# Four moves in the two-tile phase of a tiled Fourier convolution: weight group, first tile's transform, third plane operation, third tile's planes

## The chip, the cores and the metric

The kernel runs on one core of a Trainium2 chip. The metric is the device time of one execution in microseconds, as the median over several runs. The core has five engines that matter here: TensorE (PE, with PEld for its weight loads), VectorE (DVE), ScalarE (ACT), GpSimd (POOL) and SyncE (SP, which here only issues DMAs).

## The reference

An image of 224x224 pixels with 96 channels is convolved, circularly, with 7x7 taps from 96 to 96 channels. The reference does it by Fourier transforms:

```python
wp = jnp.pad(w, ((0, H - K), (0, W - K), (0, 0), (0, 0)))
Xf = rfft2(x, axes=(1, 2)); Wf = rfft2(wp, axes=(0, 1))
Yf = jnp.einsum('bhwi,hwio->bhwo', Xf, Wf)
y = irfft2(Yf, s=(H, W), axes=(1, 2)).astype(bfloat16)
```

## The kernel before, in words

**Tiling.** The kernel does not form the two-dimensional transform. Down the height it cuts the image into 8 blocks of 28 rows (two halves, `jg`, of four blocks) and transforms each block with its halo by matmuls with a matrix that it builds itself (`Fm`); that gives 17 frequencies, `s` = 0 to 16. Across the width it convolves directly, with a saving: pixels are taken in pairs, and the sums and differences of neighbouring pixels (and of real and imaginary parts) need fewer multiplications. The width is cut into 7 tiles of 32 pixels (`t` = 0 to 6).

**Stages.** For a tile: (1) the transform of its pixels to `xf`, in PSUM banks that VectorE or ScalarE evicts; (2) the planes `J`, sums and differences of `xf` on VectorE; (3) a round for each frequency s, in which TensorE multiplies planes with the transformed weights `WF`; (4) the way back, matmuls with `Gm` on data that went through a scratch in DRAM (`scr`), and the stores to the output.

**Weights.** `WF` is made from the raw weights (`wq`) in six groups of frequencies, `PGRP` = (0,2), (2,5), (5,8), and so on. `prep_jobs(gi)` (line 337) gives the jobs of a group: twelve banks of four matmuls with an eviction each, and for each inner frequency one difference on VectorE (`diff`, WF<-WF). Group 0 is made ahead of the rounds.

**A round** is `b_round(t, s, mid, end, ydve, planes)` (line 493). It takes two PSUM banks. In the first TensorE does 4, 4 and 4 matmuls (on a J plane, then on `xf` twice) and then 7 on two more J planes; those 7 read what the third plane operation wrote. ScalarE copies a part of this bank out (tt), VectorE makes `u` from the rest. Then come the `mid` jobs, 14 matmuls into the second bank, VectorE's `v` from it, the plane operations that the round was given, the sum of u and v on GpSimd (`ysum`, yf<-v,u), and the `end` jobs. For s = 0 and 16 the round is shorter (8 and 14 matmuls, no GpSimd). Where a round was given plane operations, the sum on GpSimd is made to wait for the last of them (lines 571 to 577).

**Planes.** `jit(t, g)` (line 463) gives the three VectorE operations that make the planes of the frequency group `JGB[g]` of tile t: a wide subtraction, a small addition, and an addition that reads the result of the first. They go into one of three buffers J, in turn.

**Order.** Each engine runs its instructions in the order of the program (`_Ordered`). In the two-tile phase (lines 741 to 793) round r does frequency r of tile 0 and, from r = `LAG` = 4 on, frequency r-4 of tile 1 after it; so there are 21 rounds, of up to two half rounds. Which half round gets which planes stands in `bursts`, keyed by (r, t). Other work comes in through paced queues: `add(a, b, jobs)` spreads jobs evenly over the steps a to b-1, and `pace` (line 722) pops what is due at a step. The steps are 2r for the middle and 2r+1 for the end of a round while there is one tile, and 2r and 2r+1 for tile 0's and tile 1's half rounds where there are two. Queues are served in the order in which they were added, so weight groups come first. `f_jobs(t, part)` (line 441) gives a tile's transform in three parts by frequency, s 0 to 7, 8 to 12 and 13 to 16; `fj[1][1]` and `fj[2][1]` are the upper two parts of tile 0 for the second half of its rows, 4 banks of 8 matmuls and 2 banks of 16. The engine of an eviction is chosen as the program is built, by running sums of estimated costs (`evac`, line 119).

After the two-tile phase, tiles 2 to 6 go one at a time, with the next tile's transform and the way back of earlier tiles in between.

Of the kernel before, what the change touches and what calls it, by code (L numbers as in the profile page):

```python
# [17 lines left out]
NS = L // 2  # L18
# [14 lines left out]
PGRP = ((0, 2), (2, 5), (5, 8), (8, 11), (11, 14), (14, 17))  # L33
# [6 lines left out]
JGB = ((0, 3), (3, 6), (6, 9), (9, 12), (12, 15), (15, 17))  # L40
LAG = 4
# [14 lines left out]
def kernel(  # L56
# [406 lines left out]
    def jit(t, g):  # L463
        s0, s1 = JGB[g]
        n = s1 - s0
        xf = xf_tiles[t][0:C]
        xv = xf.rearrange("c p r s w j -> c p r s (w j)")
        b = jcount[0] % 3 if t < 2 else (jcount[0] - 2 * len(JGB)) % 2
        jcount[0] += 1
        Jb = J_bufs[b][0:C].rearrange("c (k s q) -> c k s q", k=7, s=3)  # L470
        for s in range(s0, s1):
            jbuf[(t, s)] = Jb[:, :, s - s0]

        def sub(o, a, b, op, cost):
            def f():
                load["v"] += 170 + cost / 1.92
                return VE.tensor_tensor(out=o, in0=a, in1=b, op=op)
            return f
        x0, x1 = xv[:, 0, :, s0:s1], xv[:, 1, :, s0:s1]
        c0, c1 = max(s0, REAL[0] + 1), min(s1, REAL[1])  # L480
        i0, i1 = c0 - s0, c1 - s0
        pd, rd, sd, qd = x1.ap
        dpl = bass.AP(x1.tensor, x1.offset - NJ, [pd, [NJ, 2], rd, sd, qd])
        return [
            sub(Jb[:, 0:4, 0:n].rearrange("c (k r) s q -> c k r s q", r=2), dpl,
                x0.unsqueeze(1).to_broadcast([C, 2, 2, n, PP]), ALU.subtract, 4 * PP * n),
            sub(Jb[:, 4, i0:i1], xv[:, 0, 0, c0:c1], xv[:, 0, 1, c0:c1], ALU.add, PP * (c1 - c0)),
            sub(Jb[:, 5:7, i0:i1], Jb[:, 0:4:2, i0:i1], Jb[:, 1:4:2, i0:i1], ALU.add, 2 * PP * (c1 - c0)),
        ]
# [3 lines left out]
    def b_round(t, s, mid, end, ydve=False, planes=()):  # L493
# [26 lines left out]
        if s in REAL:  # L520
            for part in range(2):
                conv(b0, part * C, 0, part)
            SE.copy(out=tt_[:, 0:2 * C], in_=b0[:, 0:2 * C])
            mid()
            for mi, m in enumerate((2, 1)):
                for part in range(2):
                    conv(b1, (mi * 2 + part) * C, m, part)
            VE.tensor_tensor(out=yv.rearrange("p r m o -> p m r o"),
                             in0=tt_[:, 0:2 * C].rearrange("p (r o) -> p r o", o=C).unsqueeze(1).to_broadcast([128, 2, 2, C]),
                             in1=b1[:, 0:4 * C].rearrange("p (m r o) -> p m r o", m=2, r=2), op=ALU.add)  # L530
            load["a"] += 110 + 0.9 * 192
            load["v"] += 540
            for f in planes:
                f()
            end()
        else:
            v = tv_pool.tile([128, 2, 2, C], F32, name="v")
            if merge:
                conv(b0, 2 * C, 0, 0, both=True)
                conv(b0, 2 * C, 2, 0, add=True)  # L540
                conv(b0, 3 * C, 1, 0, add=True)
                conv(b0, 0, 0, 1)
                conv(b0, C, 0, 2)
                SE.mul(out=tt_[:], in_=b0[:, 0:4 * C], mul=-0.5)
                u, pr = tt_[:, 2 * C:4 * C].rearrange("p (m o) -> p m o", m=2), tt_[:, 0:2 * C]
            else:
                for part in range(3):
                    conv(b0, part * C, 0, part)
                conv(b0, 3 * C, 2, 0)
                conv(b0, 4 * C, 1, 0)  # L550
                u = tv_pool.tile([128, 2, C], F32, name="u")
                SE.mul(out=tt_[:, 0:3 * C], in_=b0[:, 0:3 * C], mul=-0.5)
                pr = tt_[:, C:3 * C]
            if puts:
                puts.pop(0)()
            if not merge:
                VE.scalar_tensor_tensor(out=u[:], in0=b0[:, 3 * C:5 * C].rearrange("p (m o) -> p m o", m=2), scalar=-0.5,
                                        in1=tt_[:, 0:C].unsqueeze(1).to_broadcast([128, 2, C]), op0=ALU.mult, op1=ALU.add)
            mid()
            for mi, m in enumerate((2, 1)):  # L560
                for pi, part in enumerate((1, 2)):
                    conv(b1, (mi * 2 + pi) * C, m, part)
            VE.scalar_tensor_tensor(out=v.rearrange("p m r o -> p m (r o)"),
                                    in0=pr.unsqueeze(1).to_broadcast([128, 2, 2 * C]), scalar=-2.0,
                                    in1=b1[:, 0:4 * C].rearrange("p (m q) -> p m q", m=2), op0=ALU.mult, op1=ALU.add)
            def ysum(eng):
                return eng.tensor_tensor(out=yv.rearrange("p r m o -> p m r o"), in0=v[:],
                                         in1=u.unsqueeze(2).to_broadcast([128, 2, 2, C]), op=ALU.add)
            if ydve:
                ysum(VE)  # L570
            last = None
            for f in planes:
                last = f()
            if not ydve:
                y = ysum(GE)
                if last is not None:
                    tc.add_manual_dep(y.ins, last.ins.name, SYNC, reason="sum after planes")
            load["a"] += 490 if merge else 410
            load["v"] += (560 if ydve else 250 if t < 2 else 0) + (560 if merge else 900)
            end()  # L580
# [119 lines left out]
    fj = [f_jobs(0, p) for p in range(3)]  # L700
# [37 lines left out]
    def add(a, b, jobs):  # L738
        qs.append([a, b, jobs, len(jobs)])

    for gi in range(1, len(PGRP)):
        add(2 * PGRP[gi - 1][0], 2 * PGRP[gi - 1][1] - 1, prep_jobs(gi))
    for t in range(2):
        scr_tiles[t] = dr_pool.tile([TW, NJ, NS, 4 * C], BF16, name="scr")
    bursts = {}
    for g in range(len(JGB)):
        g0 = JGB[g][0]
        if g:
            bursts[(g0 - 2, 1 if g0 - 2 >= LAG else 0)] = (0, g)
        r1 = LAG + g0 - (3 if g == len(JGB) - 1 else 1)  # L750
        bursts[(r1, 0 if r1 < NS else 1)] = (1, g)
    bursts[(NS + LAG - 2, 1)] = (2, 0)
    nburst = len(bursts)
    for r in range(NS + LAG):
        if r == 0:
            add(0, 4, fj[1][1] + fj[2][1])
        for p in range(3):
            if r == (1, 3, 5)[p]:
                new_xf(1, SH2[p], SH2[p + 1])
                fj = f_jobs(1, p)  # L760
                if p == 2:
                    for jg in range(2):
                        fj[jg][-1] = then_load(fj[jg][-1], 2, jg)
                add(2 * r + 1, 2 * r + (5, 5, 4)[p], fj[0] + fj[1])
        for p in range(3):
            if r == SH2[p + 1] + 1 - (p == 2):
                new_xf(2, SH2[p], SH2[p + 1])
                fj = f_jobs(2, p)
                if p == 2:
                    for jg in range(2):  # L770
                        fj[jg][-1] = then_load(fj[jg][-1], 3, jg)
                add(2 * r, 2 * r + (8, 7, 5)[p], fj[0] + fj[1])
        if r == PGRP[-2][1] + 1:
            assert not any(q[2] for q in qs[:len(PGRP) - 1])
            wtmp_cm.__exit__(None, None, None)
            t_pool = ctx.enter_context(tc.tile_pool(name="tt", bufs=NTT, side="right"))
            t2_pool = ctx.enter_context(tc.tile_pool(name="tt2", bufs=1, side="right"))
            yo_pool = ctx.enter_context(tc.tile_pool(name="yo", bufs=2, side="right"))
            g_pool = ctx.enter_context(tc.tile_pool(name="gp", bufs=1, side="right"))
            GA = g_pool.tile([KA, 4 * B], BF16, name="GA")  # L780
            GB = g_pool.tile([128, 2, 4 * B], BF16, name="GB")
            GE.memset(GA[:], 0.0)
            GE.memset(GB[:], 0.0)
        if r == NS + 3:
            queue_c(0)
        for t in range(2):
            s = r - LAG * t
            if not 0 <= s < NS:
                continue
            now = bursts.pop((r, t), ())  # L790
            now = jit(*now) if now else ()
            both = LAG <= r < NS
            b_round(t, s, fills(qs, 2 * r + (t if both else 0)), fills(qs, 2 * r + (t if both else 1)), False, now)
    assert not bursts and nburst == 2 * len(JGB)
    if NP2:
        ps0_cm.__exit__(None, None, None)
        ps_cms = [tc.tile_pool(name="ps", bufs=NP2, space=bass.MemoryType.PSUM),
# [108 lines left out]
```

## Time and profile before

| | us |
|---|---|
| median of 3 runs | 271.96 (271.89 to 272.75) |
| the profiled execution's own time | 272.2 |
| its span, first to last instruction | 270.5 |
| TensorE busy | 258.7 (96%) |
| VectorE busy | 213.9 (79%) |
| ScalarE busy | 195.6 (72%) |
| GpSimd busy | 95.6 (35%) |

A row of a timeline gives the start in us, the length, the engine, a line of the kernel, the operation, what it writes and reads with shapes, the number of instructions merged into the row, and in brackets the idle time of the engine before it and what ended that. All instructions carry line 88, the helper that keeps the order, so they are told apart by the names of their tiles: `pb` is a PSUM bank, `WF<-pb` a weight eviction, `WF<-WF` a difference, `J<-xf` the first two plane operations, `J<-J` the third, `u`, `v`, `yf` as above. Rows of TensorE overlap, since matmuls are pipelined.

### The profile page before, as it was taken

The page shows a single profiled execution, that of the slowest core. Times are in us where ns is not written, and L with a number is a line of the kernel's source. Part 1 is how long each engine was busy: PE and PEld are TensorE (multiplying, and loading weights), DVE is VectorE, ACT ScalarE, POOL GpSimd, SP SyncE. Part 2 cuts the span into 40 slices and gives each one's busy share as a digit, 9 for nine tenths or more (in the row PEclk, how much of TensorE's full clock was granted, in tenths as well). Part 3 has the DMA queues.
Part 4 walks back from the last instruction along what each step waited for, and adds up shares of the span by engine and source line. Part 5 has one row for each costly group of instructions (what it writes and reads, how often), then busy time and mean ns, then how long its engine had stood idle before and what let it go on. Part 6 is the DMA issues. An engine that isn't in the chain of part 4 may idle for free.

```text
span 270.5 us, 12170 instructions
## 1 busy us (share of the span) xinstructions
PE 258.7 (96%) x5149; PEld 237.8 (88%) x5149; DVE 213.9 (79%) x457; ACT 195.6 (72%) x483; POOL 95.6 (35%) x156
## 2 busy tenths in 40 slices
PE   8899998999999999999999999999999999899983
PEld 3679898999999989999999999998998989789862
DVE  5647999898889888779787888787898889778623
ACT  5549997568875657988988889887887865477113
POOL 7781032435536624431422222223222242422100
PEclk9999999999999999999999999999999999999999
DMA  6947010731121498986977477989649834887766
GB/s 168 232 124 200 23 47 2 204 105 49 43 77 63 126 276 157 292 247 177 298 206 217 116 205 244 251 210 349 222 125 163 269 103 147 200 235 203 221 118 202
DMA packets 47014, 46.78 MB, mean 173 GB/s; under 512 B 35286, under 2 KB 37986, under 8 KB 46960
## 3 DMA queue, kind: packets, MB, share of 16 engines
q1 hardware_dynamic: 44672, 43.94, 58.7%
q10 hardware_dynamic: 2288, 2.06, 2.7%
q8 instruction: 40, 0.66, 1.1%
q14 instruction: 14, 0.11, 0.2%
HBM read 24.65 MB, written 21.33 MB: 170 GB/s over the span
## 4 chain that ended last, share of the span: by engine, by line
PE 74%; DVE 7%; DMA 7%; ACT 5%; issue 3%; POOL 2%; SPq 1%; DVEq 0%; POOLq 0%; ACTq 0%
PE pb L88 74%; DMA tt<-scr 4%; ACT WF L88 3%; POOL ct L88 2%; DMA xf<-scrb 2%; DVE J L88 2%; DVE v L88 1%; DVE WF L88 1%; DVE u L88 1%; ACT xf L88 1%; DMA scrb<-yf 1%; SPq L88 1%; DVE yf L88 1%; DVE xf L88 1%; DVE wq L88 1%
## 5 line engine op out<-in xcount | busy, mean ns | idle before, releaser
L88 PE MATMUL pb<-WF,J 96*128 96x96 bf16 x2821 | 162.5, 206 | 1.1 <-DVE J L88 0.6
L88 PEld LDWEIGHTS <-J 96*128 96x128 bf16 x2821 | 138.1, 98 | 10.4 <-issue 2.6
L88 POOL TENSOR_TENSOR yf<-v,u 128x384 bf16<-128x384 f32 x79 | 78.6, 1008 | 151.7 <-issue 88.6
L88 ACT CAST xf<-pb 96x408 bf16<-96x408 f32 (+3 forms) x144 | 67.3, 486 | 8.1 <-PE pb L88 6.2
L88 PE MATMUL pb<-WF,xf 96*128 96x96 bf16 x952 | 60.2, 206 | 0.8 <-ACT xf L88 0.5
L88 DVE TENSOR_TENSOR J<-xf 96x1824 bf16<-96x1824 bf16 (+1 forms) x84 | 57.6, 724 | 0.1
L88 PEld LDWEIGHTS <-xf 96*128 96x128 bf16 x952 | 47.1, 98 | 1.2 <-ACT xf L88 0.6
L88 PE MATMUL pb<-Fm,xn 118*128 118x136 bf16 (+3 forms) x640 | 45.5, 199 | 0.9 <-DVE u L88 0.8
L88 PE MATMUL pb<-tt,Gm 102*84 102x384 bf16 (+1 forms) x132 | 32.7, 327 | 1.7 <-DMA tt<-scr 1.7
L88 ACT CAST WF<-pb 96x480 bf16<-96x480 f32 (+1 forms) x59 | 29.0, 570 | 5.7 <-PE pb L88 5.7
L88 PEld LDWEIGHTS <-xn 118*128 118x128 bf16 x640 | 30.4, 97 | 1.1 <-issue 1.1
L88 ACT CAST J<-pb 84x384 bf16<-84x384 f32 (+1 forms) x64 | 27.6, 488 | 2.4 <-PE pb L88 2.3
L88 ACT CAST yo<-pb 84x384 bf16<-84x384 f32 (+1 forms) x64 | 27.2, 482 | 1.9 <-PE pb L88 1.1
L88 DVE TENSOR_TENSOR J<-J 96x912 bf16<-96x912 bf16 (+2 forms) x42 | 22.8, 542 | 0.0
L88 PE MATMUL pb<-wq 98*128 98x120 bf16 (+1 forms) x288 | 21.3, 225 | 0.0
L88 PEld LDWEIGHTS <-wq 98*128 98x128 bf16 x288 | 19.5, 149 | 0.2
L88 PE MATMUL pb<-wu 128*128 128x512 bf16 (+1 forms) x80 | 17.6, 381 | 1.0 <-DVE ct L88 1.0
L88 PEld LDWEIGHTS <-wu 128*128 128x128 bf16 (+1 forms) x80 | 9.3, 118 | 8.2 <-issue 2.4
L88 DVE TENSOR_TENSOR yf<-v,u 128x384 bf16<-128x384 f32 x26 | 14.7, 566 | 0.9
L88 PEld LDWEIGHTS <-Gm 102*84 102x84 bf16 (+1 forms) x132 | 11.0, 117 | 2.7 <-DMA tt<-scr 2.1
L88 DVE CAST WF<-pb 96x480 bf16<-96x480 f32 (+1 forms) x13 | 7.5, 610 | 5.4 <-PE pb L88 5.3
L88 ACT COPY xf<-xf 96x816 bf16<-96x816 bf16 (+3 forms) x20 | 11.2, 618 | 0.0
(386 smaller groups left out, 233.4 us busy)
## 6 DMA issues: line engine op xcount, KB each, us to landing
scr<-yf SPq DMA_DIRECT2D x30, 288.0 KB
xn<-in_x_dram SPq DMA_DIRECT2D x12, 672.0 KB
tt<-scr SPq DMA_DIRECT2D x24, 336.0 KB
out_dram<-yo SPq DMA_DIRECT2D x12, 252.0 KB
out_dram<-J SPq DMA_DIRECT2D x12, 252.0 KB
tt<-scr SPq DMA_DIRECT2D x6, 288.0 KB
WF<-in_x_dram SPq DMA_DIRECT2D x2, 672.0 KB
out_dram<-tt SPq DMA_DIRECT2D x8, 168.0 KB
```

Source lines behind the costliest of these rows:

```text
L88: r = fn(*a, **k)
```

## The change

Four places of the two-tile phase are edited.

1. The second weight group (gi = 1, frequencies 2 to 4) is spread over two steps, 0 and 1, instead of three; the other groups keep theirs.
2. Tile 0's upper transform for the second half of the rows: the 4 banks of the middle part are spread over steps 1 to 4 and the 2 banks of the top part over steps 5 to 8, instead of all 6 over steps 0 to 3.
3. Of the three plane operations of a group, the half round that starts the group does two; the third is kept in `rest` and done at the same place of the next half round. The sum on GpSimd waits for planes only where more than one was done in its half round.
4. The planes of tile 2's first group start one round sooner: two operations in round 18 and the third in round 19, instead of all three in round 19.

```diff
             if not ydve:
                 y = ysum(GE)
-                if last is not None:
+                if len(planes) > 1:
                     tc.add_manual_dep(y.ins, last.ins.name, SYNC, reason="sum after planes")
...
     for gi in range(1, len(PGRP)):
-        add(2 * PGRP[gi - 1][0], 2 * PGRP[gi - 1][1] - 1, prep_jobs(gi))
+        add(2 * PGRP[gi - 1][0], 2 * PGRP[gi - 1][1] - (2 if gi == 1 else 1), prep_jobs(gi))
...
     bursts = {}
+    rest = []
...
-    bursts[(NS + LAG - 2, 1)] = (2, 0)
+    bursts[(NS + LAG - 3, 1)] = (2, 0)
...
         if r == 0:
-            add(0, 4, fj[1][1] + fj[2][1])
+            add(1, 5, fj[1][1])
+            add(5, 9, fj[2][1])
...
             now = bursts.pop((r, t), ())
-            now = jit(*now) if now else ()
+            now = jit(*now) if now else []
+            now, rest = rest + now[:2], now[2:]
             both = LAG <= r < NS
             b_round(t, s, fills(qs, 2 * r + (t if both else 0)), fills(qs, 2 * r + (t if both else 1)), False, now)
-    assert not bursts and nburst == 2 * len(JGB)
+    assert not rest and not bursts and nburst == 2 * len(JGB)
```

## Prediction

> **What bounds the kernel now.** I read the chain of waits, busy time by stage, then TensorE's timeline in the stretch where two tiles run together (21 to 98 us).
>
> ```profile
> PE 74%; DVE 7%; DMA 7%; ACT 5%; issue 3%; POOL 2%; SPq 1%; DVEq 0%; POOLq 0%; ACTq 0%
> ```
> ```profile
> 61.20:97.70 36.50, 35.86 (x879) 35.62 (x879) 30.71 (x63) 26.56 (x64) 19.23 (x21) 1.00 0.28 89
> 97.70:270.50 172.80, 165.43 (x3143) 152.17 (x3143) 135.03 (x289) 125.96 (x323) 49.27 (x50) 1.00 0.76 209
> ```
> TensorE makes up 74% of the chain that ends last, and its clock is 1.00. In both stretches it is busy nearly throughout (columns: length; PE, PEld, DVE, ACT, POOL; clock). The change leaves TensorE's work alone; it can only remove or add standstills. What comes after 97.7 us has the same work and order, so I carry a standstill saved before it to the end whole. The standstills (start, length, group, idle time before it and its releaser):
>
> ```profile
> 29.20 0.33 PE L88 MATMUL pb<-WF,J 96*128 96x96 bf16 x4 [0.36 <-DVE WF L88]
> 29.37 0.33 PE L88 MATMUL pb<-WF,xf 96*128 96x96 bf16 x4
> 29.89 0.33 PE L88 MATMUL pb<-WF,xf 96*128 96x96 bf16 x4 [0.19 <-DVE WF L88]
> ...
> 45.71 0.95 PE L88 MATMUL pb<-Fm,xn 118*128 118x32 bf16 x32 [0.80 <-DVE u L88]
> ...
> 57.97 0.94 PE L88 MATMUL pb<-wq 98*128 98x120 bf16 x12
> 58.75 0.93 PE L88 MATMUL pb<-WF,J 96*128 96x96 bf16 x18
> 59.52 0.50 PE L88 MATMUL pb<-WF,xf 96*128 96x96 bf16 x8
> 59.85 0.46 PE L88 MATMUL pb<-WF,J 96*128 96x96 bf16 x7
> 60.15 0.92 PE L88 MATMUL pb<-wq 98*128 98x120 bf16 x12
> 61.17 0.39 PE L88 MATMUL pb<-Fm,xn 118*128 118x64 bf16 x8
> ```
> ```profile
> 88.53 0.46 PE L88 MATMUL pb<-WF,J 96*128 96x96 bf16 x7
> ...
> 96.58 0.50 PE L88 MATMUL pb<-WF,xf 96*128 96x96 bf16 x8
> 97.70 0.94 PE L88 MATMUL pb<-WF,J 96*128 96x96 bf16 x18 [0.62 <-DVE J L88]
> ```
> Matmuls overlap: eight last 0.50, but the next group starts after 0.33 (59.52 to 59.85). So a standstill is the bracketed idle time plus about 0.16. Round 2 of tile 0 waits for its weights: 0.36+0.16 = 0.52 and 0.19+0.16 = 0.35. At 45.71 TensorE waits 0.80+0.16 = 0.96 for a PSUM bank that u frees. From 60.15 to 61.17 are 1.02 where twelve such matmuls took 0.78 before: 0.24. Tile 2's first round waits 1.12-0.33 = 0.79 for its planes. Together 2.86; smaller ones I leave out.
>
> **The change part by part.** VectorE's rows for all parts, and one of GpSimd's:
>
> ```profile
> 27.67 0.36 DVE L88 SCALAR_TENSOR_TENSOR u<-pb,tt__681 128x192 f32<-128x192 f32 x1 [1.61 <-ACT tt__681 L88]
> ...
> 29.19 1.80 DVE L88 TENSOR_TENSOR WF<-WF 96x960 bf16<-96x960 bf16 x3
> 30.90 0.55 DVE L88 SCALAR_TENSOR_TENSOR v<-tt__681,pb 128x384 f32<-128x384 f32 x1
> ...
> 39.51 2.54 DVE L88 TENSOR_TENSOR WF<-WF 96x960 bf16<-96x960 bf16 x3
> ...
> 45.32 0.34 DVE L88 SCALAR_TENSOR_TENSOR u<-pb,tt__1168 128x192 f32<-128x192 f32 x1
> ...
> 58.95 0.62 DVE L88 TENSOR_TENSOR J<-J 96x912 bf16<-96x912 bf16 x1
> 59.49 0.34 DVE L88 SCALAR_TENSOR_TENSOR u<-pb,tt__1601 128x192 f32<-128x192 f32 x1
> 59.76 0.54 DVE L88 SCALAR_TENSOR_TENSOR v<-tt__1601,pb 128x384 f32<-128x384 f32 x1
> 60.76 0.36 DVE L88 SCALAR_TENSOR_TENSOR u<-pb,tt__1662 128x192 f32<-128x192 f32 x1 [0.46 <-POOL yf L88]
> ```
> ```profile
> 39.40 1.00 POOL L88 TENSOR_TENSOR yf<-v,u 128x384 bf16<-128x384 f32 x1 [3.67 <-DVE J L88]
> ```
> ```profile
> 87.67 0.62 DVE L88 TENSOR_TENSOR J<-J 96x912 bf16<-96x912 bf16 x1
> 88.22 0.34 DVE L88 SCALAR_TENSOR_TENSOR u<-pb,tt__2546 128x192 f32<-128x192 f32 x1
> 88.48 0.53 DVE L88 SCALAR_TENSOR_TENSOR v<-tt__2546,pb 128x384 f32<-128x384 f32 x1
> ...
> 95.81 0.36 DVE L88 SCALAR_TENSOR_TENSOR u<-pb,tt__2867 128x192 f32<-128x192 f32 x1 [1.22 <-ACT tt__2867 L88]
> 96.09 0.55 DVE L88 SCALAR_TENSOR_TENSOR v<-tt__2867,pb 128x384 f32<-128x384 f32 x1
> 96.55 1.32 DVE L88 TENSOR_TENSOR J<-xf 96x1824 bf16<-96x1824 bf16 x2
> ```
> Second weight group: its fifteen jobs (twelve banks, three differences) go out 8 and 7 in two steps instead of 5, 5, 5 in three. The differences (29.19 to 30.90, 1.71 in the queue) now stand ahead of round 1's u at 27.67, before which VectorE idled 1.61. I expect them to fill that hole: u perhaps 0.3 later, everything behind them 1.71-0.3, about 1.4, earlier. Round 2 then finds its weights: 0.52+0.35 = 0.87 saved; nothing if the casts run late on ScalarE, which released that u.
>
> First tile's upper transform: the same six banks and matmuls, but one at a time from the end of round 0 to round 3 instead of all in rounds 0 and 1. TensorE does them without loss whenever they come. What is late next is their eviction, into stretches where VectorE has work without a gap. For two late banks that is 0 to 1.1 of VectorE's time (an estimate: 0.54, like v, for each). I take 0, since the lead worked out next just covers the bank wait at 45.71; at 1.1 about that wait, 0.96, would stay. No DMA hangs on these jobs; SyncE's and GpSimd's queues keep their order.
>
> Third operation, gain: on VectorE it took from 58.95 to 59.49, 0.54 of the queue, ahead of the u that frees a bank. Behind that round's v instead, it lets u go 0.54 sooner. At 45.32, u comes 1.4+0.54 = 1.94 sooner while TensorE asks 0.87 sooner, so 1.07 is there to cover 0.96: all saved (nothing, if the hole stays). The sum on GpSimd, which waits for the planes where there are two or more, also starts 0.54 sooner; that covers the 0.46 of the u at 60.76: 0.24 saved.
>
> Third operation, cost: one half round later it stands close to its reader, the seven matmuls on J. In tile 0's fourth group, v would run from 59.22, leave the queue at 59.68, and the operation end at 59.68+0.62 = 60.30; its reader stands at 59.85: 0.45 late. GpSimd also gets in the way. Three differences took 2.54 at 39.51 with a sum on GpSimd from 39.40 to 40.40, and 1.80 alone: 0.74 lost of 0.89 shared. Here tile 1's sum would run from about 59.1 to 60.1, so the operation ends near 60.65: **0.8 late**; with tile 0's sum ahead of it too, 1.75; bounds 0.45 and 1.75. Tile 1's fifth group: u from 87.68, v from 87.94, the operation from 88.40 to 89.02 against a reader at 88.53: 0.5 late, 0.7 with the rest of a sum in front, at most 1.75. I take **0.7**. The other groups have no row for the new place; each lies between 0 and the operation's own 0.62. I take 0.3 for all of them, near the low end, because the other tile's half round lies between the operation and its reader. Cost 1.8; bounds 0.95 (0.45+0.5) and 4.1 (1.75+1.75+0.62).
>
> The Trainium skill, "SBUF — State Buffer", section "Who interferes with whom", says a vector operation with two SBUF inputs and a GpSimd operation that reads SBUF exclude each other, whichever issued first holding on to its end. The row at 39.51 agrees (0.74 of 0.89). By that rule a third operation right behind v would go ahead of the sum and pay nothing itself, which no run here shows; the fourth group would then stay at 0.8, since there a sum is already running.
>
> Third tile's planes: the first two operations of tile 2, 1.32 at 96.55, move one round forward, ahead of the u at 95.81. There VectorE idles 1.22, waiting for ScalarE. So they are hidden but for 0.1, and 0.79 is saved; should the hole vanish, u and its bank slip by up to 1.32. The sum of that round then waits for them, but nothing queues behind it that tile 2's first round reads.
>
> Sum: 0.87+0.96+0.24+0.79-1.8 = 1.06 saved. The profiled execution took 272.2 (span 270.5, 1.7 around it), so 271.1; the runs' median, 271.96, is 0.24 lower, so **270.9**.
>
> **The rivals.**
> - The planes are always in time: the hand sums above put the third operation too late, because VectorE, relieved of its backlog, is ahead everywhere. For it: 1.4 saved early. Against: u at 60.76 shows VectorE waiting again later, so the lead does not last. All 2.86: 269.1.
> - The saving is handed to the next wait. For it: from 29.19 to 45.32 VectorE's rows have no gap, so TensorE, sooner at one wait, may stand longer at the next; then 0.96 and 0.24 stay and, of the other 1.66, the third operations take 1.2 to 1.8. Against: the hole of 1.61. About 271.8.
> - Slower: GpSimd's sums stand before the third operation in most groups. Two sums of 1.00 in front give 1.75 in each of the two worked groups, and the others 0.6 together: 4.1 against 2.86, 273.2. It decides once more than 2.86+0.82 = 3.7 is lost. For it: the 0.74 at 39.51, and that the order "sum after planes" no longer covers the third operation. Against: GpSimd is busy only 19.23 of 36.50. The page named above would have this only where the sum issued first.
>
> **How the numbers follow.** A measurement of this kernel tells 0.3% (0.82 us) from no change. Chances: forecast with a saving over 0.82 (to about 2.2), 0.45; all saved, 0.13; handed on, 0.27; slower, 0.15. So faster 0.58, within 0.27, slower 0.15. The range, 269.3 to 272.9, takes in the forecast, the saving handed on and the near half of the first rival; left out are the far part of it and the slower case, about 0.2.
>
> **What would show it.** Right: no idle time released by WF before round 2, none before tile 2's first J matmuls, the differences of the second group ahead of u in round 1, and new idle times released by J on the seven J matmuls of frequency 9 of tile 0 and 12 of tile 1, 0.5 to 1 long. Wrong: u before round 2 still waiting for ScalarE behind casts; the bank wait near 44 still there; sums on GpSimd lengthened instead of plane operations; or new standstills after 97.7, which I assume absent.

## The result and the profile after

The median is 270.95 us against 272.21 (22 runs each); the ratio is 0.9955, with a 95% interval of 0.994 to 0.9971. The change saves 1.26 us. The forecast was 270.9 from 271.96, a saving of 1.06. The profiled execution after took 270.2, with a span of 268.5.

Busy time by stage, first of before, then of after. The first stretch runs from TensorE's first matmul of round 0 to tile 2's first matmuls on J; I call its length the phase.

```profile
21.29:97.70 76.41, 74.21 (x1774) 73.42 (x1775) 66.78 (x130) 58.52 (x141) 30.08 (x32) 1.00 0.31 94
```
```profile
21.33:96.41 75.08, 73.96 (x1775) 73.37 (x1776) 66.02 (x128) 57.66 (x141) 32.68 (x32) 1.00 0.30 92
```

The phase went from 76.41 to 75.08: 1.33 less, which covers the difference of the medians. TensorE's busy time in it is nearly the same (74.21 and 73.96); what went is standing still. GpSimd is busy 2.6 longer (30.08 to 32.68) with the same 32 instructions; that comes back below. Each length of a phase, here and below, comes from one profiled execution.

TensorE's timeline after, the places that answer to those quoted of before:

```profile
27.73 0.34 PE L88 MATMUL pb<-WF,J 96*128 96x96 bf16 x4
27.91 0.50 PE L88 MATMUL pb<-WF,xf 96*128 96x96 bf16 x8
...
44.17 0.95 PE L88 MATMUL pb<-Fm,xn 118*128 118x32 bf16 x32 [0.18 <-DVE u L88]
...
57.99 0.50 PE L88 MATMUL pb<-WF,xf 96*128 96x96 bf16 x8
58.98 0.47 PE L88 MATMUL pb<-WF,J 96*128 96x96 bf16 x7 [0.49 <-DVE J L88]
```
```profile
82.54 0.50 PE L88 MATMUL pb<-WF,xf 96*128 96x96 bf16 x8
83.12 0.47 PE L88 MATMUL pb<-WF,J 96*128 96x96 bf16 x7
...
87.13 0.50 PE L88 MATMUL pb<-WF,xf 96*128 96x96 bf16 x8
88.01 0.47 PE L88 MATMUL pb<-WF,J 96*128 96x96 bf16 x7 [0.37 <-DVE J L88]
...
96.06 0.50 PE L88 MATMUL pb<-WF,xf 96*128 96x96 bf16 x8
96.41 0.93 PE L88 MATMUL pb<-WF,J 96*128 96x96 bf16 x18
```
Round 2 starts at 27.73 with no wait for WF, and its eight matmuls are no longer split in two fours. The wait for a bank, at 45.71 before and at 44.17 now, is down from 0.80 to 0.18 of idle time, a standstill of 0.34. Tile 2's first J matmuls follow at once (0.35 after 96.06). New are three waits for J, taken as in the prediction from start to start less 0.34: 0.99-0.34 = 0.65 before 58.98, 0.24 before 83.12, 0.54 before 88.01. They stand at frequency 9 and 15 of tile 0 and 12 of tile 1.

VectorE's timeline after, in two parts:

```profile
26.43 1.79 DVE L88 TENSOR_TENSOR WF<-WF 96x960 bf16<-96x960 bf16 x3 [0.18 <-ACT WF L88]
28.14 0.35 DVE L88 SCALAR_TENSOR_TENSOR u<-pb,tt__676 128x192 f32<-128x192 f32 x1
...
43.77 0.34 DVE L88 SCALAR_TENSOR_TENSOR u<-pb,tt__1167 128x192 f32<-128x192 f32 x1
...
57.95 0.97 DVE L88 TENSOR_TENSOR J<-J 96x912 bf16<-96x912 bf16 x1
```
```profile
63.96 0.62 DVE L88 TENSOR_TENSOR J<-J 96x912 bf16<-96x912 bf16 x1
...
94.00 1.32 DVE L88 TENSOR_TENSOR J<-xf 96x1824 bf16<-96x1824 bf16 x2
96.18 0.36 DVE L88 SCALAR_TENSOR_TENSOR u<-pb,tt__2869 128x192 f32<-128x192 f32 x1 [0.85 <-ACT tt__2869 L88]
```
The differences stand ahead of round 1's u and the hole of 1.61 is gone. Tile 2's two plane operations lie in VectorE's idle time: after them it still waits 0.85 for ScalarE. And a third operation of the same size takes 0.97 at 57.95 and 0.62 at 63.96. GpSimd's rows at these two places (three sums, two sums), and then of before two sums that ran without a plane operation beside them:

```profile
57.43 3.35 POOL L88 TENSOR_TENSOR yf<-v,u 128x384 bf16<-128x384 f32 x3 [1.41 <-issue]
```
```profile
63.09 2.35 POOL L88 TENSOR_TENSOR yf<-v,u 128x384 bf16<-128x384 f32 x2 [2.31 <-issue]
```
```profile
64.75 1.96 POOL L88 TENSOR_TENSOR yf<-v,u 128x384 bf16<-128x384 f32 x2 [2.09 <-issue]
```
At 57.95 a sum had been running since 57.43, and the operation was held. At 63.96 a sum was just ending, the operation got in ahead of the second one, kept its 0.62, and the two sums took 2.35 instead of 1.96: now the sum was held. So it goes through the whole phase: four third operations start while a sum runs and are held (57.95, 70.58, 82.41 and 86.97), three of them the ones whose readers wait, and nine sums, each behind the start of a moved third operation, take 1.17 to 1.41 instead of 1.00. That makes up most of GpSimd's 2.6.

### The profile page after: what moved, and what is told of

The parts are those of the page before. It is cut to its first block, busy times and chain, and to the rows that moved or that the text cites. A ratio compares the mean times of both kernels' runs of the same rounds, so it can differ in the third digit from the quotient of the medians.

```text
span 268.5 us, 12180 instructions
## 1 busy us (share of the span) xinstructions
PE 259.1 (97%) x5149; PEld 237.9 (89%) x5149; DVE 214.2 (80%) x457; ACT 195.2 (73%) x483; POOL 98.3 (37%) x156
## 4 chain that ended last, share of the span: by engine, by line
PE 69%; DVE 12%; ACT 7%; DMA 4%; issue 3%; POOL 2%; SPq 1%; DVEq 0%; POOLq 0%; ACTq 0%
PE pb L88 69%; DMA tt<-scr 4%; DVE J L88 4%; ACT WF L88 3%; ACT xf L88 3%; DVE v L88 2%; DVE WF L88 2%; POOL ct L88 2%; DVE u L88 1%; DVE xf L88 1%; DVE yf L88 1%; SPq L88 1%; DVE wq L88 1%; DVE tt L88 0%; DVEq L904 0%
## 5 line engine op out<-in xcount | busy, mean ns | idle before, releaser
L88 POOL TENSOR_TENSOR yf<-v,u 128x384 bf16<-128x384 f32 x79 | 81.3, 1040 | 147.8 <-issue 86.3
L88 ACT CAST xf<-pb 96x408 bf16<-96x408 f32 (+3 forms) x145 | 68.0, 493 | 9.0 <-PE pb L88 5.5
L88 DVE TENSOR_TENSOR J<-xf 96x1824 bf16<-96x1824 bf16 (+1 forms) x84 | 56.7, 714 | 0.1
L88 DVE TENSOR_TENSOR J<-J 96x912 bf16<-96x912 bf16 (+2 forms) x42 | 24.2, 577 | 0.0
L88 PE MATMUL pb<-wu 128*128 128x512 bf16 (+1 forms) x80 | 18.2, 390 | 1.0 <-DVE ct L88 1.0
```

Source lines behind the costliest of these rows:

```text
L88: r = fn(*a, **k)
```

## The experiments

Theory: the time follows TensorE's standstills in the phase, each edit has its own, and what the moved third operation costs is that its reader waits. Rivals: the standstills only show a late VectorE, so a saving at one moves to the next; or the parts need each other. I go by the phase first, because the time holds parts that no edit touches and that vary: the rounds begin between 21.29 and 21.89 in the profiles, and what follows the phase takes 171.97 to 174.53, with waits released by the DMAs tt<-scr. How well a phase repeats was not measured. A ratio is to runs of before taken alongside; their medians were 272.21 for the change, 271.98 for e1 to e4, 272.18 for e5 to e8 and 272.01 for e9 to e11.

| kernel | phase | median | ratio to before, 95% interval |
|---|---|---|---|
| before | 76.41 | | |
| all four edits | 75.08 | 270.95 | 0.9955, 0.994 to 0.9971 |
| e1: third operation in place | 74.90 | 271.74 | 0.9988, 0.9966 to 1.001 |
| e2: third operation alone | 77.07 | 273.28 | 1.0048, 1.003 to 1.0066 |
| e3: weights alone | 75.18 | 271.44 | 0.9965, 0.9939 to 0.9991 |
| e4: upper transform as before | 74.85 | 270.7 | 0.9943, 0.9919 to 0.9966 |
| e5: third operation ahead of v | 78.01 | 274.11 | 1.0064, 1.0033 to 1.0095 |
| e6: the same, upper transform as before | 77.88 | 273.86 | 1.0054, 1.003 to 1.0077 |
| e7: three groups in place | 73.71 | 269.32 | 0.9885, 0.9848 to 0.9923 |
| e8: sum behind the third operation | 79.77 | 275.46 | one execution |
| e9: three in place, upper transform as before | 73.46 | 269.47 | 0.9903, 0.9875 to 0.9932 |
| e10: weights and third tile's planes | 74.42 | 270.43 | 0.9936, 0.9912 to 0.996 |
| e11: third tile's planes alone | 75.67 | 273.24 | one execution |

**e1, the third operation in its old place**, the other three edits kept.

```diff
-                if len(planes) > 1:
+                if last is not None:
...
-            now = jit(*now) if now else []
-            now, rest = rest + now[:2], now[2:]
+            now = jit(*now) if now else ()
```


> The other three edits, with the third plane operation back in its old place and the sum on GpSimd waiting for it again. Mark: the start of tile 2's first matmuls on J, 97.70 before and 96.41 with all four edits. Theory (the move costs more in readers that wait than it gives back): the three standstills released by J at 58, 83 and 87 (0.66, 0.24, 0.53) are gone, the bank wait near 44 grows from 0.34 to about 0.9, and some 0.4 of small waits near 60 and 71 return: mark near 95.95, time about 0.4 to 0.5 below that of all four edits. Rival (the move pays for itself, because u comes 0.54 sooner after every group): the bank waits return in more places, mark at or above 96.4, time equal to or above that of all four.

TensorE's timeline of this kernel near the bank wait:

```profile
45.63 0.53 PE L88 MATMUL pb<-Fm,xn 118*128 118x32 bf16 x15 [0.79 <-DVE u L88]
```
The three waits for J are gone, and the bank wait is 0.79+0.16 = 0.95, as long as before the change. The phase is 0.18 shorter, not 0.46: two waits of 0.20, near 37 and 41, stand there beside the small ones that were expected. So across all twelve groups the move pays back nearly what it costs, and the rival was half right. The median did not follow (271.74). The rounds began at 21.89 in its profile, 0.56 later than with all four; whether they do so in every execution the runs don't tell, so which of the two is faster stays open.

**e2, only the third operation moved.** Before, with the two lines on `now`, `rest` and the condition on the sum:

```diff
-            now = jit(*now) if now else ()
+            now = jit(*now) if now else []
+            now, rest = rest + now[:2], now[2:]
```


> Only the third plane operation is moved; weights, first tile's transform and tile 2's planes as before. Theory: the same three standstills of 1.4 in all, and one of about 1.2 on the seven J matmuls of round 3, since without the earlier differences v of round 2 leaves VectorE only at 34.6; gains of about 1.0 (0.54 of the bank wait, 0.24 and 0.19 of the small ones). Mark near 99.3, that is 0.5 to 0.6% slower than before. Rival (the move pays for itself): mark at or below 97.7, no slower than before.

TensorE's timeline, round 3:

```profile
33.62 0.50 PE L88 MATMUL pb<-WF,xf 96*128 96x96 bf16 x8
34.73 0.47 PE L88 MATMUL pb<-WF,J 96*128 96x96 bf16 x7 [0.60 <-DVE J L88]
```
Slower, by 0.48%, as the theory has it. Round 3 waits 0.77, not 1.2, and the waits at frequency 9, 15 and 12 are 0.65, 0.23 and 0.53, as with all four edits. The phase grew 0.66 where 1.6 was expected, since the bank wait of 0.96 went altogether and not by half. The median grew by more, 1.30, and one more wait, just behind the phase, fits that: tile 2's third operation, moved too, starts at 98.92 behind a sum, takes 1.07 instead of 0.46, and TensorE waits 0.41+0.16 = 0.57 for it before 100.06.

**e3, only the weights sooner.**

```diff
-        add(2 * PGRP[gi - 1][0], 2 * PGRP[gi - 1][1] - 1, prep_jobs(gi))
+        add(2 * PGRP[gi - 1][0], 2 * PGRP[gi - 1][1] - (2 if gi == 1 else 1), prep_jobs(gi))
```


> Only the second weight group comes sooner. Theory: the waits for WF before round 2 (0.87) go, and the three differences fill VectorE's hole of 1.61 ahead of round 1's u, so that about half of the bank wait of 0.96 goes too: mark near 96.3, time 1.3 to 1.5 lower than before; tile 2's wait of 0.79 stays. Rival (the weights need the room that the first tile's upper transform leaves): the casts queue behind the transform's evictions, the wait for WF shrinks by half at most, mark above 97.1.

```profile
44.54 0.63 PE L88 MATMUL pb<-Fm,xn 118*128 118x32 bf16 x19 [0.71 <-DVE u L88]
```
This row of TensorE's timeline is the bank wait: 0.71+0.16 = 0.87, hardly less than 0.96. The waits for WF are gone without any room from the transform, so that rival falls. The phase is 1.23 shorter: 0.87 at round 2, 0.27 of a wait for WF near 41, and 0.09 at the bank. Edit 1 alone yields nearly all that the four yield together.

**e4, the first tile's upper transform as before**, the other three edits kept.

```diff
-            add(1, 5, fj[1][1])
-            add(5, 9, fj[2][1])
+            add(0, 4, fj[1][1] + fj[2][1])
```


> All edits but that of the first tile's upper transform, whose six banks stay in steps 0 to 3. Theory (that edit moves work that TensorE does without loss anyway): no wait for WF, mark within 0.5 of 96.41, and a wait for J in round 3 of at most 0.6. Rival (that edit makes the room): a wait for WF of 0.4 or more stays before round 2, mark above 96.9.

```profile
43.12 0.92 PE L88 MATMUL pb<-wq 98*128 98x120 bf16 x12
43.88 0.96 PE L88 MATMUL pb<-Fm,xn 118*128 118x32 bf16 x32
```
In TensorE's timeline the bank wait is gone (0.76 from start to start, the time of twelve such matmuls), no wait for WF returns, and round 3 waits 0.28 for J. The phase is 0.23 shorter. So edit 2 costs a little. That its two late banks are evicted where VectorE has no room is not shown by itself: the u that frees the bank starts at 43.77 with the edit and at 43.36 without it, but with the edit VectorE also idles 0.44 for ScalarE before the u at 34.34.

**e5, the third operation between u and v** of the next half round, all four edits kept.

```diff
-    def b_round(t, s, mid, end, ydve=False, planes=()):
+    def b_round(t, s, mid, end, ydve=False, planes=(), first=()):
...
+            for f in first:
+                f()
             mid()
...
-            now, rest = rest + now[:2], now[2:]
+            third, now, rest = rest, now[:2], now[2:]
```
The last line of the loop hands `third` to `b_round` as `first`.


> All four edits, but the third plane operation goes between u and v of the next half round instead of behind v. Measure: the two-tile phase, from TensorE's first matmuls on tile 0 to tile 2's first on J: 76.4 before, 75.1 with all four edits. Theory (what the third operation costs is that its reader waits for it): it ends 0.5 to 0.9 sooner; the three standstills released by J (0.66, 0.24, 0.53) shrink to 0.2 or less in all, the bank wait of 0.34 stays: phase 73.7 to 74.0, time 1.0 to 1.4 below that of all four edits. Rival (VectorE's queue is what costs, wherever the operation stands): v and the bank that it frees come 0.5 to 1.0 later, and waits for banks of as much appear instead: phase 74.8 or more.

At the place of 57.95 above, one row each of VectorE, GpSimd and TensorE:

```profile
58.54 1.42 DVE L88 TENSOR_TENSOR J<-J 96x912 bf16<-96x912 bf16 x1
```
```profile
58.48 0.99 POOL L88 TENSOR_TENSOR yf<-v,u 128x384 bf16<-128x384 f32 x1 [1.41 <-issue]
```
```profile
60.02 0.47 PE L88 MATMUL pb<-WF,J 96*128 96x96 bf16 x7 [0.93 <-DVE J L88]
```
My theory failed here: the phase is 2.9 longer than with all four, not 1.2 shorter. The operation stands 0.46 sooner behind its u, without v between them, but there it starts 0.06 after a sum, which runs from 58.48 to 59.47; it ends at 59.96, half a microsecond after it. It takes 1.42 instead of 0.97, and its reader stands 0.93+0.16 = 1.09. Six of the third operations take 1.38 to 1.43 in this way. The waits for J grew to 1.1, 0.64 and 1.1, which is 1.4 of the 2.9. The rest is mostly five new waits of 0.2 to 0.4 for xf, WF and a bank (near 37, 40, 54, 72 and 81): what stands in VectorE's queue behind a held operation is late too. So the rival had the sign and, in these later waits, a share of the cost; that they follow from the held operations is argued here, not shown by a run of its own.

**e6** is e5 with the edit of e4:

```diff
-            add(1, 5, fj[1][1])
-            add(5, 9, fj[2][1])
+            add(0, 4, fj[1][1] + fj[2][1])
```

> As the run before, with the first tile's upper transform back in steps 0 to 3. Theory: that edit costs 0.2 of the phase (75.1 against 74.9 in the pair measured first), so the phase is 73.4 to 73.8 and the time about 0.2 below the run before. Rival (the upper transform's place matters more once nothing waits for J): a wait for WF or a bank of 0.3 or more in rounds 1 to 3, phase at or above that of the run before.

77.88 against 78.01: the upper transform is worth 0.13 here, and round 3 waits 0.25 for WF. Both phases are far above the expected ones for the reason seen in e5.

**e7, three groups keep the third operation with the other two**: those whose readers waited.

```diff
-            now = bursts.pop((r, t), ())
+            now = key = bursts.pop((r, t), ())
             now = jit(*now) if now else []
-            now, rest = rest + now[:2], now[2:]
+            n = 3 if key in ((0, 3), (0, 5), (1, 4)) else 2
+            now, rest = rest + now[:n], now[n:]
```


> All four edits, but three groups (tile 0's fourth and sixth, tile 1's fifth), the ones whose readers waited, keep the third operation with the other two. Theory: those standstills (1.43) go, and about 0.25 of the bank wait near 60 comes back: phase 73.8 to 74.0, time 1.1 to 1.3 below that of all four. Rival (a standstill there only stands for VectorE being late, and moves to the next wait): phase 74.8 or more, with bank waits of about 0.5 near 59 and 88.

TensorE's list of waits over the whole span (released by, us in total, times, longest):

```profile
PE pb L88 <- DMA tt<-scr: 1.1, 3, 0.7
PE pb L88 <- DVE ct L88: 1.1, 1, 1.1
PE pb L88 <- DMA wq<-in_w_dram: 0.7, 1, 0.7
PE pb L88 <- ACT xf L88: 0.5, 1, 0.5
PE pb L88 <- DVE u L88: 0.2, 1, 0.2
```
No wait for J or WF is left that this list counts, and one for u, the bank near 44 (0.21+0.16 = 0.37). The phase is 73.71, 1.37 less than with all four: the three standstills (1.43) went and did not move on. The ratio is 0.9885 against 0.9955, and the intervals do not touch: this version beats both kernels. Against e1, where all twelve groups are in place, the nine moved ones together save 74.90-73.71 = 1.19; the three cost about as much as these nine bring. How the 1.19 is shared among the nine was not tried; the one held at 70.45 takes 0.99 here, and no reader waits for it.

**e8, the sum of the half round that starts a group waits for the third operation too**, so that no sum runs beside it. The sum is kept in a list and issued after the third operation.

```diff
+    late = []
...
+            while late:
+                y = late.pop()(GE)
+                tc.add_manual_dep(y.ins, last.ins.name, SYNC, reason="sum after planes")
-            if not ydve:
+            if not ydve and t < 2 and len(planes) > 1 and s != y1 - 1:
+                late.append(ysum)
+            elif not ydve:
```


> All four edits, but the sum on GpSimd of the half round that starts a group waits for the third operation too, one half round later, so that no sum runs while the third operation does. Theory (a running sum holds the third operation up): the operation takes 0.62 instead of 0.97 in tile 0's fourth and tile 1's fifth group and 0.30 instead of 0.65 in tile 0's sixth, and the standstills released by J shrink from 0.66, 0.53 and 0.24 to about 0.3, 0.2 and 0. Rival (it is long for another reason): 0.97 and 0.65 stay.

VectorE's timeline at the same place:

```profile
59.83 0.62 DVE L88 TENSOR_TENSOR J<-J 96x912 bf16<-96x912 bf16 x1
61.65 0.36 DVE L88 SCALAR_TENSOR_TENSOR u<-pb,tt__1662 128x192 f32<-128x192 f32 x1 [1.19 <-POOL yf L88]
```
The operation takes 0.62, as expected: with no sum beside it, it has its length. But u now waits 1.19 for the late sum, and the standstills did not shrink: 0.74 at frequency 9, and new ones before WF and banks; the phase is 79.77. So running side by side costs less than keeping them apart in this way.

**e9** is e7 with the same edit on top:

```diff
-            add(1, 5, fj[1][1])
-            add(5, 9, fj[2][1])
+            add(0, 4, fj[1][1] + fj[2][1])
```

> Three groups keep the third operation in its old place, as in the run that gave a phase of 73.7, and the first tile's upper transform goes back to steps 0 to 3. Theory (that edit only moves evictions into VectorE's full stretch): the bank wait of 0.37 near 44 goes too, phase 73.3 to 73.6, time 0 to 0.4 below the run with three groups in place. Rival (the edit makes room for the weights): a wait for WF or J of 0.3 or more in rounds 1 to 3, phase 73.9 or more.

The bank wait is gone, round 3 waits 0.21 for J, and the phase is 73.46, 0.25 less than in e7. In time the two cannot be told apart.

**e10, weights and third tile's planes only**: the diff of e3 and

```diff
-    bursts[(NS + LAG - 2, 1)] = (2, 0)
+    bursts[(NS + LAG - 3, 1)] = (2, 0)
```

> Only the second weight group sooner and the third tile's planes a round sooner. Theory (the two are independent): 76.42 less 1.24 (weights alone, measured) less 0.79: phase 74.4, the bank wait near 44 stays at about 0.9. With the third operation and the first tile's transform both as before this should be 0.5 below the run with the third operation in place (74.9). Rival (the upper transform's place is needed): phase 74.9 or more. Time about 1.5 to 2 below before.

74.42 was measured where 74.4 was worked out from e3 and the wait at tile 2. With edit 2 added (e1) it is 74.90: that edit costs 0.48 here. Two of the four edits, without the others, give a phase 0.66 shorter than all four; in time, 0.9936 against 0.9955 with intervals that overlap, the two cannot be told apart.

**e11, the third tile's planes alone**, for the size of that part: before, with the last diff only.

```diff
-    bursts[(NS + LAG - 2, 1)] = (2, 0)
+    bursts[(NS + LAG - 3, 1)] = (2, 0)
```

> Only the third tile's planes a round sooner. Theory: the wait of 0.79 at tile 2's first matmuls on J goes and nothing else moves: phase 75.6, all other standstills as before. Rival (the two operations, 1.32, do not fit into VectorE's idle time of 1.22 and push u and its bank): phase 76.0 or more, with a wait for a bank or for J in rounds 19 and 20.

```profile
96.63 0.50 PE L88 MATMUL pb<-WF,xf 96*128 96x96 bf16 x8
96.97 0.93 PE L88 MATMUL pb<-WF,J 96*128 96x96 bf16 x18
```
In TensorE's timeline tile 2's J matmuls follow 0.34 after the ones on xf, so its wait is gone; the phase is 75.67, 0.74 less, and the other standstills are as before. The single time, 273.24, is no lower than before's: after the phase this execution took 174.53, 1.73 more than before. Two waits for tt<-scr (1.32 and 1.61) stand out there, but they explain little of it: TensorE is not busy for 174.53-166.90 = 7.63 of that stretch, and was not for 172.80-165.43 = 7.37 before. It is busy 1.47 longer, and its granted clock was 0.83 from 230 to 240 us, where before's was 1.00. What lowered the clock was not tried, so this one time says nothing on the edit.

## Why the prediction was right, point by point

- **Weights**: 0.87 forecast at round 2, 0.87 found (e3). Beyond it e3 saved 0.27 near 41, which I had left out as small. VectorE's lead was over-rated: without the third operation moved, the bank wait stayed at 0.87 to 0.95 (e3, e1), so the hole of 1.61 bought hardly any of the 0.96 there.
- **First tile's upper transform**: taken as 0, with the remark that at 1.1 of VectorE's time the bank wait would stay. This is the step that failed, though it is a small one: the edit costs 0.23 (e4), 0.13 (e6), 0.25 (e9) and 0.48 (e10), each from one pair of phases and all of one sign. The 0.34 left of the bank wait is there with the edit and not without it (e4).
- **Third operation, gain**: 0.96 and 0.24 forecast. The bank wait went down by 0.62 and the one at 60.15 went. That it was the move and not the lead which did this is shown by e2, where the bank wait vanished by the move alone.
- **Third operation, cost**: 0.8 forecast at the fourth group, 0.65 found; 0.7 and 0.54 at tile 1's fifth; 0.3 for all others, 0.24 found, all of it at tile 0's sixth group. In all 1.8 against 1.43. The places and the mechanism held; e7 shows that these waits were nearly the whole cost (1.37 of 1.43).
- **Third tile's planes**: 0.79 forecast, 0.74 found (e11).
- **The sum**: a saving of 1.06, against 1.33 of the phase and 1.26 of the median. The cost was over-rated by 0.37 and two small waits (0.27 and 0.19) went that I had left out; against that, 0.34 of the bank wait stayed. With these the sum would be 1.55, and the 0.2 by which the phase falls short of it was not traced. So the parts partly made up for each other, and that 270.9 lies within 0.1 of the median is also luck: before's median over 22 runs is 0.25 above the one that the forecast started from.
- **The rivals**: "always in time" falls with the three waits for J. "Handed to the next wait" shows in one place, the bank near 44; otherwise e3, where the waits for WF went and the phase fell by as much, and e7 refute it. "Slower" did not happen with the change, but e5 shows that its mechanism can decide: what a third operation pays depends on whether a sum started before it. The rule of the Trainium skill ("SBUF — State Buffer", "Who interferes with whom"), that whichever issued first holds on, is what the rows show both ways: 0.62 with the sum held (63.96), 0.97 and 1.42 with the operation held (57.95, e5).
- **The signs**: all that were named for "right" are there, with 0.65 and 0.54 for the two new waits for J. But two of those named for "wrong" are there in part as well: 0.34 of the bank wait near 44, and nine lengthened sums. The sums were lengthened beside plane operations, four of which were held, and not instead of them.

## What to carry to other kernels

When a group of operations is split and its last part moved, look up each reader by itself: three of these twelve had readers that waited, the other nine together gained, and the sum of all hid both. Where two engines exclude each other, a place that is earlier can be worse, because it may start just behind the other engine's operation; read from the timeline what will be running there. Measure an edit of one stage by that stage's length in the trace when the run's time varies by as much as the edit is worth.

## What the hardware showed that was not expected

The exclusion works in both directions. The forecast read one of them off its rows, VectorE held at 39.51; the other stands in the trace of before as well, in GpSimd's and VectorE's timelines:

```profile
88.43 2.62 POOL L88 TENSOR_TENSOR yf<-v,u 128x384 bf16<-128x384 f32 x2 [1.60 <-issue]
```
```profile
89.41 1.73 DVE L88 TENSOR_TENSOR J<-xf 96x1216 bf16<-96x1216 bf16 x2
```
These two sums took 2.62, with two plane operations beside the second one, where two sums without them took 1.96. The change made this the usual case. After it a third operation that came first kept 0.62, and two sums of together 1.96 took 2.35; in e5 one that came 0.06 after a sum took 1.42, which is the sum's 0.93 still to run and about half a microsecond. Over the phase GpSimd's busy time grew from 30.08 to 32.68 with no instruction added.
